# Attention with normed q and k, then a two-layer MLP: where the scratch columns of batch 2's last Newton roots stand

## The chip, the cores and the metric

One core of a Trainium2 chip runs the kernel. The metric is the device time of one launch in microseconds (us); less is better. The engines are named as in the profile: PE (matrix products), PEld (its weight loads), DVE (vector), ACT (activations), POOL, SP (issues transfers). PSUM is the memory into which PE writes its products and from which DVE and ACT read them.

## The reference, cut to what matters

```python
def _attn_ref(q, k, v, g_q, g_k):                    # q, k, v: 8 batches, 12 heads, 448 x 64
    rmsnorm = lambda x, g: x / np.sqrt(np.mean(x * x, axis=-1, keepdims=True) + 1e-06) * g
    q_n, k_n = rmsnorm(q, g_q), rmsnorm(k, g_k)
    scores = 1.0 / np.sqrt(64) * np.matmul(q_n, k_n.transpose(0, 1, 3, 2))
    attn = np.exp(scores - np.max(scores, axis=-1, keepdims=True))
    attn = attn / (np.sum(attn, axis=-1, keepdims=True) + 1e-09)
    return np.matmul(attn, v)

def _moe_ref(x, w_in, w_out):                        # x: 3584 x 768, w_in: 768 x 2048, w_out: 2048 x 768
    h = x @ w_in
    g = 0.5 * h * (1.0 + np.tanh(np.sqrt(2.0 / np.pi) * (h + 0.044715 * h * h * h)))
    return g @ w_out
```

The part around the change is `rmsnorm`: each row of 64 numbers of q and k needs the reciprocal root of its mean square.

## The kernel before, in words

The eight batches go through a software pipeline. For a batch b there are: loads of raw q and k; squares (`square`, L157) and their sums over 64 (`total`, L170); reciprocal roots; the normed q and k (`normed`, L273); their transposes; the attention itself (`attention`, L584, for three chunks c of four heads each, seven steps t per chunk: scores, exponentials, sums, products with v); the first layer (x times w_in and the gelu) and the second layer (g times w_out). In the loop at L925 the pass b does batch b's first layer and then the attention of batch b + 1, between whose steps the second layer of earlier batches is woven in by the hand-written orders `STEADY` and `SECOND` (L571 to L582). All instructions stand in the order in which the code issues them (`manual_schedule`), one in-order queue for each engine.

**The ring of PSUM tiles.** `rounds` holds tiles of 128 x 2 x 512 numbers, that is, two banks of 512 columns. There are two of them at first and four after the attention's start-up (L1022). `pair` (L70) takes the first tile of the list, puts it at the list's end and returns it, so `rounds[-1]` is the tile that was handed out last. Products use the first S = 448 columns of each of the two banks; columns 448 to 511 are not written by them. Every score, sum, product and first-layer step takes its tile from this ring, so a tile taken for something else moves all later ones by a place. `steady()` is true once the ring has four tiles.

**The first layer in steady state** goes by `mm1_turn` (L523). A pair i of 128-column blocks of w_in has one tile of the ring, and its 48 products on 64 x 64 quarters of PE come in two turns (which half of the contraction goes to which bank), and each turn in an early part (cs 0 to 3, 16 products) and a late part (cs 4 and 5, 8 products). When both turns have ended, one gelu on ACT (L543) reads the tile. For batch 1 the order of PE's work is: at the end of `attention(1)` (L678 to L685) the early parts of pairs 0, 1 and 2, both turns, 96 products in all; then in the loop at f == 1 and f == 3 (L991 to L996) the late parts of pairs 0 and 1, 32 products; then at f == 5 (L997 to L1000) the late part of pair 2's turn 1, 8 products, all of pair 3's turn 0, 24 products, and the late part of pair 2's turn 0, 8 products. Pairs 4 to 7 follow, two turns each.

**The last roots.** Most reciprocal roots are made on ACT. `rsqrt_last` (L243) makes those of a batch's last chunk on DVE instead: from 28 mean squares per partition a first guess by integer arithmetic (L255), and three Newton steps of four instructions (L259 to L262), 14 DVE instructions with L254. They run on y (in SBUF), t (in SBUF) and on z and u, two operands of 28 columns that stand in PSUM. It is called twice: for batch 1 before the ring has four tiles (L934), where z and u lie in unused columns of another tile (`oall[0]`), and for batch 2 in steady state (L966), in the loop's slot f == 0 of batch 1's first layer, after the sums of chunk 2 (L965). POOL then makes the normed q and k of chunk 2 with these roots, and SP transposes them.

Before the change, the call for batch 2 takes a tile of the ring for itself, `pair("root")`, and puts z and u side by side in the first columns of its bank 0.

Of the kernel before, what the change touches and what calls it, by code (L numbers as in the profile page):

```python
# [17 lines left out]
def kernel(  # L18
# [12 lines left out]
    B, H, S, D = q.shape  # L31
# [34 lines left out]
    rounds = [  # L66
        ps_t.tile([128, 2, 512], F32, tag=f"t{i}", name=f"t{i}") for i in range(2)
    ]

    def pair(name):  # L70
        rounds.append(rounds.pop(0))
        return rounds[-1]
# [3 lines left out]
    def steady():  # L76

        return bool(late_on)
# [100 lines left out]
    oall = [ps_o.tile([128, 512], F32, tag=f"o{r}", name=f"o{r}") for r in range(2)]  # L179
    roots, places = {}, {}  # L180

    def place(b, c):
        if (b, c) == (0, NCH - 1):
            t = ps_m.tile([128, 512], F32, tag="mm", name="root")[:, :4 * NT]
        else:
            i = c % 2 * 4 * NT
            t = oall[1][:, S + i:S + i + 4 * NT]
        roots["qk", b, c] = t.rearrange("p (n a t) -> p n a t", n=2, a=2)
        for n in range(2):
            roots.setdefault(("qk"[n], b, c), roots["qk", b, c][:, n])  # L190
        return t
# [51 lines left out]
    def rsqrt_last(b):  # L243


        c, flat, m = slice(NCH - 1, NCH), "p c n a t -> p (c n a t)", 4 * NT
        y, ms = rinvs[b][:, c].rearrange(flat), sss[b][:, c].rearrange(flat)
        if steady():
            own, dst = pair("root")[:, 0], y
        else:  # L250
            own, dst = oall[0][:, S:], place(b, 1)
        z, u = own[:, :m], own[:, m:2 * m]
        t = smp.tile([P, NCH * 4 * NT], F32, tag="lg", name="lg")[:, :m]
        nc.vector.tensor_scalar(u, ms, 1.0 / D, 1e-6, op0=ALU.mult, op1=ALU.add)  # L254
        nc.vector.tensor_scalar(  # L255
            y.bitcast(I32), u.bitcast(I32), -0.5, float(0x5F3759DF), op0=ALU.mult, op1=ALU.add
        )
        for i in range(3):
            nc.vector.tensor_copy(z, y)  # L259
            nc.vector.tensor_mul(t, z, y)  # L260
            nc.vector.scalar_tensor_tensor(z, t, -0.5, u, op0=ALU.mult, op1=ALU.mult)
            nc.vector.scalar_tensor_tensor(  # L262
                y if i < 2 else dst, z, 1.5, y, op0=ALU.add, op1=ALU.mult
            )
# [660 lines left out]
    for b in range(B):  # L925
        m1, side, extra, ends = [], [], [], []
        if b == 0:
# [4 lines left out]
                   lambda: normed(1, 0, "k", nc.gpsimd)),  # L932
                  (2, lambda: total(1, 1, "q"), lambda: total(1, 1, "k"),
                   lambda: normed(1, 0, "q", nc.vector), lambda: rsqrt_last(1),  # L934
                   lambda: normed_both(1, 1, nc.vector)),
                  (6, lambda: trans(1, 0, nc.scalar)),
# [23 lines left out]
        elif b + 1 < B:  # L960

            m1.append((0, lambda: gpsimd_waits(ess[b, NCH - 1][:1, 0, 0, :1])))
            for c in range(NCH):
                if b == 1 and c + 1 == NCH:
                    m1 += [(0, lambda: total(2, 2, "q")), (0, lambda: total(2, 2, "k")),  # L965
                           (0, lambda: rsqrt_last(2))]  # L966
                m1 += [(0, lambda c=c: normed_both(b + 1, c, nc.gpsimd)),
                       (4 * c + 4, lambda c=c: transposed(b + 1, c))]
            m1 += [(9, lambda: gain(b + 1, 0)), (14, lambda: gain(b + 1, 1))]
# [13 lines left out]
        for f in range(nf // 2 if b == 0 else nf):  # L983
            i, part = f // 4 * 2, f % 4
# [71 lines left out]
```

## Time and profile before

| what | us |
|---|---|
| median of 3 runs | 391.18 |
| lowest and highest of them | 391.13, 391.48 |
| the profiled execution's own time | 391.23 |
| its span, first to last instruction | 389.2 |
| PE busy in the span | 380.6 |
| ACT busy | 278.7 |
| DVE busy | 235.9 |
| POOL busy | 126.3 |

The span leaves out what lies before the first and behind the last instruction, here 391.23 - 389.2 = 2.0 us. In rows of the timeline stand: start, duration, engine, line, operation, tiles written <- read, shapes, number of instructions, and in brackets the idle time before and what ended it. Rows of the chain have start, duration and what ran. Starts are us from the span's start. PE runs four products on quarters of its array at a time, so the durations of single products overlap.

### The profile page before, as it was taken

The page shows a single profiled execution, that of the slowest core. Times are in us where ns is not written, and L with a number is a line of the kernel's source. Part 1 is how long each engine was busy: PE and PEld are TensorE (multiplying, and loading weights), DVE is VectorE, ACT ScalarE, POOL GpSimd, SP SyncE. Part 2 cuts the span into 40 slices and gives each one's busy share as a digit, 9 for nine tenths or more (in the row PEclk, how much of TensorE's full clock was granted, in tenths as well). Part 3 has the DMA queues.
Part 4 walks back from the last instruction along what each step waited for, and adds up shares of the span by engine and source line. Part 5 has one row for each costly group of instructions (what it writes and reads, how often), then busy time and mean ns, then how long its engine had stood idle before and what let it go on. Part 6 is the DMA issues. An engine that isn't in the chain of part 4 may idle for free.

```text
span 389.2 us, 17542 instructions
## 1 busy us (share of the span) xinstructions
PE 380.6 (98%) x8060; PEld 294.0 (76%) x8060; DVE 235.9 (61%) x366; ACT 278.7 (72%) x353; POOL 126.3 (32%) x110
## 2 busy tenths in 40 slices
PE   7899999999999999999999999999999999999996
PEld 4565577877887788877888788877888778887664
DVE  5998938976596359836589257953598204980010
ACT  6995499767994689757995589946897449944300
POOL 5996506384005440093103740064300900000000
PEclk9999999999999999999999999999999999999999
DMA  8999999999614992379822995159631721120033
GB/s 266 322 231 211 210 230 263 223 200 264 113 44 100 243 213 58 80 132 217 194 65 65 214 227 103 45 110 251 108 80 50 125 44 42 44 65 4 2 83 81
DMA packets 64446, 54.68 MB, mean 141 GB/s; under 512 B 37620, under 2 KB 60020, under 8 KB 64372
## 3 DMA queue, kind: packets, MB, share of 16 engines
q1 hardware_dynamic: 53936, 41.33, 43.8%
q0 software_dynamic: 10128, 11.80, 18.5%
q8 instruction: 63, 1.03, 1.1%
q10 hardware_dynamic: 308, 0.43, 0.4%
q14 instruction: 11, 0.09, 0.1%
HBM read 45.61 MB, written 11.01 MB: 146 GB/s over the span
## 4 chain that ended last, share of the span: by engine, by line
PE 92%; ACT 5%; DMA 1%; issue 1%; DVE 0%; POOL 0%; DVEq 0%
PE t L537 33%; PE t L495 32%; PE t L387 9%; PE t L335 7%; PE t L463 5%; ACT ex L343 4%; PE t L556 4%; DMA rawq<-in_q_dram 1%; PE h L436 1%; PE tp L296 1%; PE o L387 0%; POOL nrmq L278 0%; ACT g L543 0%; DVE ss L173 0%; ACT sq L162 0%
## 5 line engine op out<-in xcount | busy, mean ns | idle before, releaser
L343 ACT ACTIVATE ex<-t,shift 128x896 bf16<-128x896 f32 x168 | 156.2, 1016 | 1.9 <-PE t L335 1.6
L495 PE MATMUL t<-wout,g 64*64 64x384 bf16 (+1 forms) x3456 | 150.6, 305 | 0.0
L537 PE MATMUL t<-xT,win 64*64 64x448 bf16 x2688 | 128.7, 349 | 0.3 <-ACT g L543 0.3
L495 PEld LDWEIGHTS <-g 64*64 64x64 bf16 x3456 | 112.9, 107 | 19.2
L537 PEld LDWEIGHTS <-win 64*64 64x64 bf16 x2688 | 96.6, 107 | 31.0 <-issue 0.5
L543 ACT ACTIVATE g<-t 128x896 bf16<-128x896 f32 x56 | 50.5, 915 | 57.1 <-PE t L537 57.1
L173 DVE TENSOR_REDUCE ss<-sq 128x14 f32<-128x896 f32 (+3 forms) x45 | 44.5, 997 | 51.9 <-ACT sq L162 49.1
L335 PE MATMUL t<-qT,kT 64*64 64x448 bf16 x672 | 58.2, 351 | 1.4 <-ACT ex L343 0.6
L799 POOL COPY mark<-es 1x1 bf16<-1x1 bf16 x7 | 1.2, 177 | 132.0 <-DVE es L362 128.3
L355 DVE TENSOR_TENSOR es<-ex 128x1792 bf16<-128x1792 bf16 x20 | 21.2, 1061 | 33.0 <-ACT ex L343 33.0
L278 POOL TENSOR_TENSOR nrmq<-rawq,rinv 128x896 bf16<-128x896 f32 (+1 forms) x21 | 34.9, 1660 | 18.6 <-ACT rinv L205 11.0
L278 POOL TENSOR_TENSOR nrmk<-rawk,rinv 128x896 bf16<-128x896 f32 (+1 forms) x21 | 34.4, 1640 | 0.0
L387 PE MATMUL t<-ex,vb 64*64 64x448 bf16 x588 | 31.9, 350 | 0.0
L335 PEld LDWEIGHTS <-kT 64*64 64x64 bf16 x672 | 25.5, 106 | 7.3 <-DVE kT L305 1.2
L397 DVE STREAM_TRANSPOSE st<-t 128x448 f32<-128x448 f32 x42 | 24.7, 626 | 9.7 <-PE t L387 9.7
L387 PEld LDWEIGHTS <-vb 64*64 64x64 bf16 x672 | 23.5, 107 | 7.3 <-issue 1.0
L409 DVE STREAM_TRANSPOSE rb<-rc 128x896 f32<-128x896 f32 (+1 forms) x25 | 26.7, 1068 | 0.3
L705 DVE COPY osb<-t 128x384 f32<-128x384 f32 (+1 forms) x4 | 2.0, 507 | 35.2 <-PE t L463 35.2
L422 DVE TENSOR_TENSOR xT<-t,rb 128x896 bf16<-128x896 f32 x21 | 22.8, 1087 | 0.8
L164 POOL TENSOR_TENSOR sq<-rawq 128x896 f32<-128x896 f32 (+1 forms) x9 | 13.6, 1513 | 28.6 <-DVE ss L173 27.3
L513 ACT COPY osb<-t 128x768 f32<-128x768 f32 (+1 forms) x18 | 12.6, 701 | 13.9 <-PE t L495 13.9
L358 DVE TENSOR_TENSOR es<-es,ex 128x1792 bf16<-128x1792 bf16 x20 | 21.3, 1063 | 0.7 <-ACT ex L343 0.6
(103 smaller groups left out, 313.5 us busy)
## 6 DMA issues: line engine op xcount, KB each, us to landing
rawq<-in_q_dram SPq DMA_DIRECT2D x22, 448.0 KB, 5.0
rawk<-in_k_dram SPq DMA_DIRECT2D x22, 448.0 KB, 5.8
out_dram<-osb SPq DMA_DIRECT2D x42, 192.0 KB, 2.7
vb<-in_v_dram POOLq DMA_DIRECT2D x6, 672.0 KB, 7.3
win<-in_moe_w_in_dram POOLq DMA_DIRECT2D x8, 384.0 KB, 10.8
wout<-in_moe_w_out_dram POOLq DMA_DIRECT2D x3, 768.0 KB, 17.1
out_dram<-osb SPq DMA_DIRECT2D x24, 96.0 KB, 3.7
vb<-in_v_dram POOLq DMA_DIRECT2D x2, 448.0 KB, 15.5
```

What stands on the lines that cost most here:

```text
L173: nc.vector.reduce_sum(sss[b][:, seat(b, c), "qk".index(n), hs, ts], squares(b, c, n, hs, ts), axis=AX.X)
L278: eng.tensor_mul(nrms[n, b, c][:, ts].rearrange("p t a d -> p a t d"), raws[n, b, c][:, :, ts], root[:, :, ts].to_broadcast([P, 2, m, D]),)
L335: nc.tensor.matmul(sc[r * R:(r + 1) * R, a, :S], kT[rs, c, t, r], qT[b][rs, c, :, r], start=True, stop=True,)
L343: nc.scalar.activation(exs[b, c][:, t], scs.pop((b, c, t))[:, :, :S], AF.Exp, scale=scale, bias=shift)
L358: nc.vector.tensor_add(es, es, ex[:, 4:6])
L387: nc.tensor.matmul(o[r][a * D:(a + 1) * D], vb[b % 2][rs, 2 * c + a, i] if what else ones[rs], es[i][rs, a], start=(i == 0), stop=(i == n ...
L397: nc.vector.transpose(st[:, r].rearrange("p a b -> p (a b)"), o[r])
L409: nc.vector.transpose(oas["rb"][:, rs].rearrange("p r s -> p (r s)"), rc.to_broadcast([128, (rs.stop - rs.start) * m, 32]),)
L422: nc.vector.tensor_mul(xT[b][:, 2 * c:2 * c + 2], oas["o", c, 1][:, :, :S], oas["rb"])
L495: mm = nc.tensor.matmul(o[a * R:(a + 1) * R, bank, :hi - lo], g[rs, f, at:at + R], wout[rs, f, lo:hi], start=(n == 0), stop=(n == len(step ...
L537: mm = nc.tensor.matmul(h[a * R:(a + 1) * R, j, :S], win[rs, c, at:at + R], xT[b][rs, c], start=begin and c == cs[0], stop=end and c == cs ...
L543: nc.scalar.activation(g[:, 2 * i:2 * i + 2, (b % 2) * S:(b % 2 + 1) * S], h[:, :, :S], AF.Gelu_apprx_tanh,)
```

## The change

In `rsqrt_last`, for the call in steady state: no tile is taken from the ring. z stands in columns 448 to 475 of bank 0 and u in columns 448 to 475 of bank 1 of `rounds[-1]`, the tile that was handed out last. The ring is not turned, so the tile that the roots had taken before goes to the next user. The other branch computes the same places as before. The 14 DVE instructions, their number and their shapes stay. The change adds one line, so the lines behind it have numbers greater by one in the changed kernel.

```diff
         if steady():
-            own, dst = pair("root")[:, 0], y
+            z, u = (rounds[-1][:, i, S:S + m] for i in range(2))
+            dst = y
         else:
-            own, dst = oall[0][:, S:], place(b, 1)
-        z, u = own[:, :m], own[:, m:2 * m]
+            z, u = oall[0][:, S:S + m], oall[0][:, S + m:S + 2 * m]
+            dst = place(b, 1)
         t = smp.tile([P, NCH * 4 * NT], F32, tag="lg", name="lg")[:, :m]
         nc.vector.tensor_scalar(u, ms, 1.0 / D, 1e-6, op0=ALU.mult, op1=ALU.add)
```

## Prediction

> **What bounds the kernel now.** I read the page first: its head, the busy shares and the chain that ended last.
>
> ```profile
> span 389.2 us, 17542 instructions
> PE 380.6 (98%) x8060; PEld 294.0 (76%) x8060; DVE 235.9 (61%) x366; ACT 278.7 (72%) x353; POOL 126.3 (32%) x110
> PE 92%; ACT 5%; DMA 1%; issue 1%; DVE 0%; POOL 0%; DVEq 0%
> ```
>
> PE is busy for 98% of the span and makes 92% of the chain. So a microsecond that PE loses counts in full if it isn't given back later, and work that DVE loses counts only through PE. That is an average, so the next view is PE's own waits from 82 us on, and then a window that runs from 82.62 us to the end.
>
> ```profile
> PE t L537 <- ACT g L543: 0.3, 1, 0.3
> 82.62:389.15 306.53, 302.87 (x6848) 241.90 (x6847) 169.45 (x228) 214.42 (x266) 75.64 (x53) 1.00 0.53 114
> 385.49:389.15 3.66, 0.00 (x0) 0.00 (x0) 0.36 (x1) 0.00 (x0) 0.00 (x0) 1.00 0.41 108
> ```
>
> In the first row are the total, the number and the longest of PE's waits: one wait, of 0.3 us, for a gelu, in the whole rest of the kernel. In the other two, the columns behind the length are the busy time of PE, PEld, DVE, ACT and POOL, then the granted clock, the DMA share and GB/s. PE is busy for 302.87 us from 82.62 us on and for none of the last 3.66 us: 306.53 - 3.66 = 302.87, so it has no idle time between 82.62 and 385.49 us. A delay of PE at 82 us meets nothing later that could absorb it. The one wait and the change are in the same place, the first layer of batch 1, so I went there next, in narrow windows of the timeline.
>
> ```profile
> 81.60 0.58 PE L537 MATMUL t<-xT,win 64*64 64x448 bf16 x8
> 81.65 0.92 ACT L543 ACTIVATE g<-t 128x896 bf16<-128x896 f32 x1 [2.45 <-PE t L537]
> 81.79 0.58 PE L537 MATMUL t<-xT,win 64*64 64x448 bf16 x8
> ...
> 81.98 0.39 PE L537 MATMUL t<-xT,win 64*64 64x448 bf16 x4
> ...
> 82.62 0.38 PE L537 MATMUL t<-xT,win 64*64 64x448 bf16 x4 [0.26 <-ACT g L543]
> ```
>
> Products start in groups of four, one on each quarter of PE, and a group follows the last by 0.19 us: 81.60, 81.79, 81.98. Each lasts 0.39 us, so two groups overlap. The next group should start at 81.98 + 0.19 = 82.17 and starts at 82.62: **PE loses 0.45 us**, though only 0.26 us of it shows as idle. It is pair 3, whose tile is the one that pair 0 had, and pair 0's gelu ends at 81.65 + 0.92 = 82.57. PE starts 0.05 us later.
>
> The run of first-layer products before that wait has 136 of them:
>
> ```profile
> 75.73 6.63 PE L537 MATMUL t<-xT,win 64*64 64x448 bf16 x136
> ```
>
> By the code these are the 96 early ones of pairs 0, 1 and 2, the 32 late ones of pairs 0 and 1, and last the 8 of pair 2's turn 1: 96 + 32 + 8 = 136. The last two groups, which start at **81.79** and 81.98, are therefore pair 2's turn 1.
>
> **The change part by part.** *The ring isn't turned.* Pair 3 gets the tile that the roots had before, and no gelu stands in its way. This removes the wait of 0.45 us. The tiles of pairs 4 and 5 also come one user later and pair 6 now takes pair 2's tile, behind pair 2's gelu; by the code 120 products lie between pair 2's last and pair 6's first, so by 0.048 us each (6.63 / 136, rounded down) there are 5.8 us for a gelu of 0.92 us. From pair 7 on the ring is the same up to names. Cost of all this: nothing.
>
> *The scratch moves to a tile in use.* `rounds[-1]` is then pair 2's tile, handed out at the end of `attention(1)`, with its early parts done and its late parts to come. Its columns 448 to 475 are written by no product. What decides is whether the program orders DVE and PE nevertheless. The listing of the built programs answers that. In the old one pair 2's turn 1 waits for nothing and pair 3 waits for ACT; in the new one:
>
> ```
> 2410 L538 Matmult t3_893<-xT_1310,win_119 64x448 [waits DVE_49]
> ...
> 2426 L538 Matmult t1_101<-xT_1310,win_119 64x448
> ```
>
> The first row is the first of pair 2's last 8 products (t3), the second the first product of pair 3 (t1), which now waits for nothing. The count for which the first waits is that of the last Newton instruction, L262 (L263 in the new numbering). The first Newton instruction in turn waits for pair 2's early products.
>
> That the order is by bank and not by column is what the Trainium skill asks for ("PSUM — Partial Sum Buffer", section "PSUM bank collisions raise a hardware error"): two engines in one bank and one quarter of its partitions at once are an error even at different columns, so it says to guard "by bank × quadrant, not by address". It speaks against this change: columns that no product uses are no separate place. By columns alone the sum would be -0.45 us, by the bank it is the one below. No run here shows the collision itself; the built program follows the rule.
>
> *When do the roots end?* The timeline of DVE:
>
> ```profile
> 80.17 1.07 DVE L173 TENSOR_REDUCE ss<-sq 128x14 f32<-128x896 f32 x1
> 81.28 0.19 DVE L254 TENSOR_SCALAR t<-ss 128x28 f32<-128x28 f32 x1
> 81.51 0.19 DVE L255 TENSOR_SCALAR rinv<-t 128x28 int32<-128x28 int32 x1
> ...
> 84.19 0.18 DVE L262 SCALAR_TENSOR_TENSOR rinv<-t,rinv 128x28 f32<-128x28 f32 x1
> ```
>
> The 14 instructions start 0.22 us apart, from 81.28 to 84.19, and the last ends at 84.37. They can't start earlier: the sum over the last squares ends at 80.17 + 1.07 = 81.24. Nor does their own new wait delay them: pair 2's early products are the 96th of 136 and end at about 75.73 + 96 x 0.048 + 0.3 = 80.6 us, 0.7 us before 81.28. A second wait in front of one instruction costs DVE's queue an extra semaphore instruction; L422 has such ones:
>
> ```profile
> L422 DVEq EVENT_SEMAPHORE  x8: 21/21/848, 64.0 to 347.5; - x8
> ```
>
> 0.02 us, the median. That z and u are in two banks instead of one is not shown in the trace. The same instructions with their operands in another PSUM tile, for batch 1, are the nearest rows:
>
> ```profile
> L254 DVE TENSOR_SCALAR o<-ss x1: 181/181/181, 42.5 to 42.5; 128x28 f32<-128x28 f32 x1
> L254 DVE TENSOR_SCALAR t<-ss x1: 191/191/191, 81.3 to 81.3; 128x28 f32<-128x28 f32 x1
> ```
>
> 10 ns between two places in PSUM. For 14 instructions that is up to 0.14 us either way; I take 0, as the other forms differ by nothing like as much, and keep -0.14 and +0.14 for the range.
>
> *What the new wait costs.* The time from the end of a DVE instruction to a product that waited for it is in these rows:
>
> ```profile
> 17.36 0.56 DVE L278 TENSOR_TENSOR nrmk<-rawk,o 128x384 bf16<-128x384 f32 x1
> ...
> 17.97 0.23 PE L296 MATMUL tp<-ident,nrmk 128*128 128x128 bf16 x1 [0.48 <-DVE nrmk L278]
> ```
>
> 17.97 - 17.92 = 0.05 us. So pair 2's last 8 products start at 84.37 + 0.02 + 0.05 = 84.44 us instead of 81.79. PE's queue is in order, so everything behind them on PE waits too. Pair 3 follows two groups later, at 84.44 + 2 x 0.19 = 84.82, instead of 82.62. **The sum: 84.82 - 82.62 = +2.20 us** (2.65 us of stall, less the 0.45 us that the ring gave back). From there PE's order is the old one without idle time, so it ends 2.20 us later, and with it the last copies and stores.
>
> What else is late: pair 2's gelu (old start 84.38 us) and, behind it in ACT's queue, the squares for batch 3. ACT has time: it is busy for 214.42 of the 306.53 us. What hangs on DVE and POOL alone, the normed q and k of batch 2's last chunk and their transposes, stays where it is and is 2.2 us early against PE. That opens no new wait, and there was none on PE to close.
>
> So the profiled execution's 391.23 us become 393.43. It stands 0.05 us above the median of the runs shown, 391.18; against that the forecast is 393.4 us.
>
> **The rivals.**
>
> *The wait doesn't hold PE (the other side).* If the roots were through before PE reaches pair 2's last 8 products, or the wait were met otherwise, only the ring's gain would be left: 391.2 - 0.45 = 390.8 us. It decides at 81.79 us: the last Newton instruction would have to end 2.6 us earlier than it did. Against it stands that the first one starts at 81.28, behind a sum that ends 0.04 us before, in a chain of 0.22 us steps. For it: nothing but a wait that counts something else than I read. I give it 3 in 100. It comes out within 0.2%.
>
> *PE comes back at a lower clock.* The stall leaves PE idle from 81.98 us, the end of the group of 81.60, to 84.44, that is 2.46 us. If the granted clock fell for it, the products behind would go at half pace for a while. Taken as long as the longest idle time in the rows above, 3.66 us, half pace loses 1.83 us: 393.4 + 1.8 = 395.2 us. Against it: in the row from 385.49 us PE is idle for 3.66 us at a granted clock of 1.00 throughout. I give it 5 in 100. The Trainium skill ("TensorE: Matmul & The Clock Gate", section "Why this matters for your kernels") warns of idle gaps over about 3 us, as one window of 3.4 us without work halves the clock; by its figure the loss would be an estimated 1.7 us. Our gap is under that, and the trace's row leans the same way.
>
> *Part is given back.* Products behind the stall could go closer together, if small waits are now hidden under overlapping products. The chain of work shows their pace before and behind the old wait:
>
> ```profile
> 75.93 5.70 PE t L537 x120
> ...
> 82.62 11.92 PE t L537 x248
> ```
>
> 47.5 and 48.1 ns each: 0.15 us at most in this stage, and PE's other stages have no idle time either. With 0.3 us given back it is 393.1 us. I give it 7 in 100; it lies in the range.
>
> **How the numbers follow.** Forecast 85 in 100, 393.4 us. Its own range is 393.0 to 393.9: 0.14 us for the place of the operands, 0.35 us for the distance between the lowest and highest run shown. The range goes from 392.8, where some is given back, to 394.2, part of the way to a lower clock. A measurement of this kernel can tell about 0.2% from no change, 0.8 us. Slower by more than that: the forecast, the lower clock and the part given back, 85 + 5 + 7 = 97, less 1 for a return large enough to hide it: 96. The 4 that are left are that return and the case without a wait; 3 of them lie within 0.2% of no change, and 1 is for a gain by more, faster.
>
> **What would show it.** Right: in the changed profile PE has one wait of about 2.5 us at 82 us, of L538 for DVE's L263; pair 3 starts near 84.8 us without a wait for a gelu; the 14 DVE instructions stand between 81.3 and 84.4 us with the same lengths; from there on PE has no idle time and ends near 387.7 us, in a span near 391.4; the clock stays at 1.00. Wrong: PE reaches 82.17 us without a stop (no wait held it), or the Newton chain itself starts later or takes longer than 3.1 us, or PE's products behind the stall run at a pace other than 48 ns, or PE waits again for ACT or DMA behind 85 us.

## The result, and the profile after

The changed kernel takes **393.62 us** (median of 4 runs, 393.21 to 394.08) against 391.16 us (4 runs, 391.13 to 391.48): ratio **1.0061**, 95% interval 1.0044 to 1.0079. It is slower by 2.5 us, and the whole interval is above 0.2%. The profiled execution took 393.56 us, 2.33 us more than the profiled one before, and its span grew by 391.5 - 389.2 = 2.3 us.

The page of the changed kernel, its head, the busy shares and the chain that ended last:

```profile
span 391.5 us, 17544 instructions
PE 381.1 (97%) x8060; PEld 293.3 (75%) x8060; DVE 236.2 (60%) x366; ACT 278.9 (71%) x353; POOL 126.3 (32%) x110
PE 89%; ACT 5%; DVE 3%; DMA 1%; issue 1%; POOL 0%; DVEq 0%
```

The work is the same: as many products, DVE and ACT instructions. Two instructions more are the semaphore waits that precede the first DVE instruction of the roots and the gelu of pair 2. DVE, which had 0% of the chain, now makes 3% of it. PE's waits from 20 us on:

```profile
PE t L538 <- DVE rinv L263: 2.5, 1, 2.5
PE t L336 <- ACT ex L344: 0.3, 1, 0.3
```

The wait for the gelu (L537 for L543, now L538 for L544) is gone, and one for the last Newton instruction stands in its place. The timeline around it:

```profile
79.22 2.07 DVE L173 TENSOR_REDUCE ss<-sq 128x14 f32<-128x896 f32 x2
...
81.40 0.19 DVE L255 TENSOR_SCALAR t<-ss 128x28 f32<-128x28 f32 x1
...
84.30 0.18 DVE L263 SCALAR_TENSOR_TENSOR rinv<-t,rinv 128x28 f32<-128x28 f32 x1
84.54 2.81 PE L538 MATMUL t<-xT,win 64*64 64x448 bf16 x53 [2.52 <-DVE rinv L263]
```

The 14 instructions of the roots start 0.22 us apart as before. The last ends at 84.48, and pair 2's last 8 products start 0.06 us later. The bracket says that PE had been idle for 2.52 us. The chain shows what follows:

```profile
84.08 0.20 DVE t L262
84.30 0.20 DVE rinv L263
84.54 12.30 PE t L538 x256
96.84 0.81 PE t L496 x20
```

256 products in 12.30 us, 48 ns each, and then the second layer: pair 3 starts without a wait, and the pace is the old one. A window from there to the end and one behind PE's last product (busy times of PE, PEld, DVE, ACT, POOL, then granted clock, DMA share, GB/s):

```profile
84.54:391.45 306.91, 303.25 (x6856) 241.27 (x6855) 167.97 (x220) 213.20 (x264) 75.45 (x52) 1.00 0.51 113
387.79:391.45 3.66, 0.00 (x0) 0.00 (x0) 0.36 (x1) 0.00 (x0) 0.00 (x0) 0.81 0.41 108
```

306.91 - 3.66 = 303.25: no idle time of PE in between, so nothing gives the loss back. The second row has a clock of 0.81 where the same idle stretch at the end of the kernel before showed 1.00. That turns out to matter.

### The profile page after: what moved, and what is told of

Read it like the earlier page. It is cut to its first block, busy times and chain, and to the rows that moved or that the text cites. A ratio compares the mean times of both kernels' runs of the same rounds, so it can differ in the third digit from the quotient of the medians.

```text
span 391.5 us, 17544 instructions
## 1 busy us (share of the span) xinstructions
PE 381.1 (97%) x8060; PEld 293.3 (75%) x8060; DVE 236.2 (60%) x366; ACT 278.9 (71%) x353; POOL 126.3 (32%) x110
## 4 chain that ended last, share of the span: by engine, by line
PE 89%; ACT 5%; DVE 3%; DMA 1%; issue 1%; POOL 0%; DVEq 0%
PE t L496 32%; PE t L538 31%; PE t L388 8%; PE t L336 7%; PE t L464 5%; ACT ex L344 4%; PE t L557 4%; DVE ss L173 1%; DMA rawq<-in_q_dram 1%; PE h L437 1%; DVE xT L423 1%; PE tp L297 1%; PE o L388 0%; DVE rb L410 0%; DVE st L398 0%
## 5 line engine op out<-in xcount | busy, mean ns | idle before, releaser
L538 PE MATMUL t<-xT,win 64*64 64x448 bf16 x2688 | 128.7, 349 | 2.5 <-DVE rinv L263 2.5
L538 PEld LDWEIGHTS <-win 64*64 64x64 bf16 x2688 | 96.1, 107 | 33.7 <-issue 2.8
L544 ACT ACTIVATE g<-t 128x896 bf16<-128x896 f32 x56 | 50.5, 915 | 59.3 <-PE t L538 59.3
L336 PE MATMUL t<-qT,kT 64*64 64x448 bf16 x672 | 58.1, 351 | 1.4 <-ACT ex L344 0.6
L336 PEld LDWEIGHTS <-kT 64*64 64x64 bf16 x672 | 25.4, 106 | 7.5 <-DVE kT L306 1.5
```

The costliest lines, as they stand in the source:

```text
L336: nc.tensor.matmul(sc[r * R:(r + 1) * R, a, :S], kT[rs, c, t, r], qT[b][rs, c, :, r], start=True, stop=True,)
L538: mm = nc.tensor.matmul(h[a * R:(a + 1) * R, j, :S], win[rs, c, at:at + R], xT[b][rs, c], start=begin and c == cs[0], stop=end and c == cs ...
L544: nc.scalar.activation(g[:, 2 * i:2 * i + 2, (b % 2) * S:(b % 2 + 1) * S], h[:, :, :S], AF.Gelu_apprx_tanh,)
```

## The experiments

Some executions, of the kernel before too, take one to three microseconds longer than the rest without a lower clock. In two profiled executions (pair 3 ahead, and the changed kernel once more) the trace has a late transfer: DVE waits 1.7 to 1.8 us, until about 63.5 us, for a transpose into kT, and PE then waits 1.5 us in L336 for DVE's L142. That the others have the same cause is not shown. Medians are given with the lowest time where this blurs them. The ratios come with their intervals and are not the quotients of the two medians, from which they can differ a little.

**The place of the scratch alone.** The ring is turned as before the change:

```diff
             z, u = (rounds[-1][:, i, S:S + m] for i in range(2))
+            pair("root")
```

Expected: 

> The changed kernel, but the ring is turned by one tile after the roots have taken their place, as it was before the change: only the place of the scratch differs from the kernel before. Theory (PE is held at pair 2's last 8 products until the last Newton step ends): the gain of the ring, 0.45 us, lies behind the stall and can't be seen, so the time is that of the changed kernel, 393.4 to 393.7 us, with one wait of PE of 2.5 us. Rival one (the loss comes from the new order of tiles in the ring): 391.2 us. Rival two (stall and ring add up): 393.6 + 0.45 = 394.1 us.

Measured: 394.15 us (393.52 to 395.31, 6 executions) against 391.30, ratio 1.0067 (1.0043 to 1.0091). Four executions had a mean granted clock of 0.998 to 1.000 and took 393.52 to 394.52 us; two had 0.994 and 0.995 and took 394.98 and 395.31. The first group fits the wait, with the ring's gain hidden behind it (one execution, of 394.52 us, lies above the expectation, nearer to rival two; the trace has one wait of 2.5 us and none for the gelu beside it); the ring's order is not the cause. The second group was in no theory. Its profiled execution, in windows cut at the changes of the clock:

```profile
81.55:84.96 3.41, 0.90 (x24) 0.48 (x19) 2.47 (x14) 2.19 (x3) 1.65 (x2) 1.00 0.89 233
84.96:88.37 3.41, 3.41 (x44) 2.22 (x40) 0.00 (x0) 0.24 (x1) 2.98 (x2) 0.50 1.16 290
88.37:91.79 3.42, 3.42 (x80) 2.57 (x75) 1.60 (x2) 2.87 (x5) 0.00 (x0) 1.00 1.14 250
```

The column behind POOL is the granted clock: **0.50 for 3.41 us** right after the stall, with 44 products in it where the next window of the same length has 80. The chain of the same execution gives the price:

```profile
84.52 13.98 PE t L539 x256
```

13.98 - 12.30 = 1.68 us for the same 256 products.

**The ring alone.** The scratch goes to SBUF:

```diff
-            z, u = (rounds[-1][:, i, S:S + m] for i in range(2))
+            z, u = (smp.tile([P, m], F32, tag=n, name=n) for n in ("zz", "uu"))
```

Expected: 

> The ring's part alone: no tile is taken from the ring, and z and u are two small tiles in SBUF. Theory: no instruction of PE waits for the roots, and pair 3 doesn't wait for pair 0's gelu: 391.2 - 0.4 = 390.8 us, PE without a wait behind 20 us. Rival (the order of tiles in the ring costs the time): 393.6 us. If the Newton steps are slower in SBUF beside POOL (0.2 to 0.4 us each instead of 0.22), the roots come up to 2.5 us later and nothing waits for them on PE: still 390.8 us.

Measured: 391.09 us (lowest 390.51, 12 executions) against 391.30 (lowest 391.04), ratio 0.9995 (0.9976 to 1.0014): no loss, and the gain is not told from no change by the times. The trace shows it. PE's only wait behind 20 us, and the chain:

```profile
PE t L336 <- ACT ex L344: 0.3, 1, 0.3
```

```profile
75.78 18.16 PE t L538 x384
93.94 0.81 PE t L496 x20
```

The whole first layer of batch 1, 384 products, goes without a stop at 47 ns each, in 18.16 us. In the kernel before it went from 75.93 to 82.62 + 11.92 = 94.54 us by its chain, 18.61 us: the ring's part is 0.45 us.

**The scratch in the next tile of the ring** (pair 3's) instead of the last:

```diff
-            z, u = (rounds[-1][:, i, S:S + m] for i in range(2))
+            z, u = (rounds[0][:, i, S:S + m] for i in range(2))
```

Expected: 

> The changed kernel with the scratch columns in the tile that the ring hands out next (pair 3's) instead of the one handed out last. Theory (a wait by tile, whatever the columns): now pair 3's first product waits for the last Newton step; PE gets to it at 82.2 us and is let go at 84.5 us, where it started at 82.62 before: 391.2 + 1.9 = 393.1 us, the stall 0.4 us shorter than in the changed kernel. Rival (only a tile with half-made sums in it is held): 390.8 us. Rival (the ring's order): 393.6 us.

Measured: 394.77 us (394.53 to 394.92, 5 executions) against 391.30, ratio 1.0079 (1.0057 to 1.0101): missed by 1.7 us. The wait is as expected, 2.1 us (first fence: PE's waits, the row for L538), and so the tile that is held needn't have half-made sums in it. What the expectation lacks is the clock, at 0.995 or 0.996 in four of the five executions:

```profile
PE t L538 <- DVE rinv L263: 2.1, 1, 2.1
```

```profile
82.26:85.67 3.41, 1.34 (x32) 0.95 (x31) 1.82 (x10) 1.60 (x3) 1.72 (x2) 1.00 0.90 231
85.67:89.09 3.42, 3.42 (x44) 2.29 (x40) 1.08 (x1) 2.15 (x4) 2.19 (x2) 0.50 1.37 193
```

```profile
84.45 13.61 PE t L538 x248
```

The kernel before makes these 248 products in 11.92 us: 1.69 us are the clock's, and without them the profiled execution's 394.53 would be 392.84, near the 393.1 expected. The fifth execution took 394.92 us at a clock of 0.999; it has no profile, and why it took so long stays open.

**Pair 3 ahead of pair 2's rest:**

```diff
-                mm1_turn(b, 2, 1, late)
                 mm1_turn(b, 3, 0, range(HP), begin=True)
+                mm1_turn(b, 3, 1, range(HP), end=True)
+                mm1_turn(b, 2, 1, late)
                 mm1_turn(b, 2, 0, late, end=True)
...
-            elif part == 3:
+            elif part == 3 and (b, f) != (1, 7):
```

Expected: 

> The changed kernel, with all 48 products of pair 3 issued ahead of pair 2's last 16. Theory (the release is a fixed time, set by DVE): PE gets to pair 2's products 48 x 0.048 = 2.3 us later, at 84.1 us, and is let go at 84.5 us: a stall of 0.4 us, as long as the old wait for the gelu, so 391.2 us. Rival (the stall has its own length of 2.5 us wherever it stands, or the ring's order costs the time): 393.6 us.

Measured: 391.56 us (eleven executions 391.35 to 391.84, one 393.11) against 391.30, ratio 0.9998 (0.9985 to 1.0011). With 2.3 us of other products in front, the stall of 2.5 us is gone: it is a fixed time at which PE is let go. The profiled execution is the one of 393.11, with the late transfer, which moves everything behind it; this is its row among PE's waits:

```profile
PE t L336 <- DVE rawk L142: 1.5, 1, 1.5
```

PE's products in this kernel, in narrow windows of the timeline:

```profile
84.39 0.39 PE L538 MATMUL t<-xT,win 64*64 64x448 bf16 x4
84.84 0.38 PE L538 MATMUL t<-xT,win 64*64 64x448 bf16 x4
85.62 0.55 PE L538 MATMUL t<-xT,win 64*64 64x448 bf16 x8
86.15 0.38 PE L538 MATMUL t<-xT,win 64*64 64x448 bf16 x4
86.34 0.38 PE L538 MATMUL t<-xT,win 64*64 64x448 bf16 x4
86.79 0.38 PE L538 MATMUL t<-xT,win 64*64 64x448 bf16 x4
```

Groups should follow by 0.19 us. Twice they follow by 0.45 (84.39 to 84.84, 86.34 to 86.79): there a pair changes its turn with no other pair's products between, and the second turn waits until the first is finished (`follows` in `mm1_turn` orders them), for 0.26 us each. In between, at 86.15, is what is left of the wait for the roots. So this order buys the stall back, and pays for it in turns.

**Two, and four, Newton steps** in the changed kernel (with two, the third step of the roots is left out), and four in the kernel before. The diff is that for two steps; the other two kernels have 4 in the place of the 2 in its first line:

```diff
-        for i in range(3):
+        for i in range(2 if steady() else 3):
...
-                y if i < 2 else dst, z, 1.5, y, op0=ALU.add, op1=ALU.mult
+                y if i < 2 or steady() else dst, z, 1.5, y, op0=ALU.add, op1=ALU.mult
```

Expected of two: 

> The changed kernel with two Newton steps instead of three for batch 2's last roots (the third step is left out). Theory of the wait: PE is let go four instructions of 0.22 us earlier, 0.89 us, so 393.5 - 0.9 = 392.6 us, PE idle for 1.6 us. Theory of the clock (a span of 3.41 us that is more than about half idle is followed by as long a span at half clock, as in the traces of e1_turned and e3_nexttile): 1.6 us is under half of 3.41, so no execution pays for it, and the runs lie close together. Rival (any stall of PE lowers the clock): 392.6 + 1.5 = 394.1 us. Rival (the stall isn't what costs the time): 393.6 us.

Expected of four: 

> The changed kernel with four Newton steps. Theory of the wait alone: 393.5 + 0.9 = 394.4 us. With the theory of the clock: PE is idle for 3.4 us, as long as one span of the clock's, so wherever those spans begin one of them is at least half idle, and most executions have 3.4 us at half clock, which cost 1.4 us more (as between the runs of e1_turned with and without): 395.8 us. Rival (the stall isn't what costs the time): 393.6 us.

Expected of four in the kernel before: 

> The kernel before the change with four Newton steps instead of three for the same roots. Theory: PE waits for none of these instructions, and the normed q and k of that chunk have time, so nothing changes: 391.2 us. Rival (the length of the roots' chain costs time by way of POOL and the transposes, whatever tile they use): 392.1 us.

Measured: with two 392.62 us against 391.26 (12 executions, all at a clock of 0.998 or more), ratio 1.0032 (1.0015 to 1.0049); with four 396.22 us (5 executions, all at 0.994 to 0.996), ratio 1.0129 (1.0096 to 1.0161); the kernel before with four 391.27 against 391.26 us, ratio 0.9993 (0.9977 to 1.001). The same four instructions cost 0.9 us of waiting (PE's wait is 1.6, 2.5 and 3.4 us with two, three and four steps) or nothing, by whether PE waits for them. The waits of PE in the first two, and the windows of the clock:

```profile
PE t L538 <- DVE rinv L263: 1.6, 1, 1.6
```

```profile
81.08:84.49 3.41, 1.79 (x43) 1.12 (x36) 2.30 (x11) 2.19 (x3) 2.54 (x3) 1.00 0.77 166
84.49:87.90 3.41, 3.41 (x80) 2.57 (x76) 0.50 (x1) 1.91 (x4) 2.78 (x2) 1.00 1.51 280
```

```profile
PE t L538 <- DVE rinv L263: 3.4, 1, 3.4
```

```profile
82.15:85.57 3.42, 0.24 (x8) 0.19 (x11) 2.65 (x15) 1.63 (x3) 0.77 (x2) 1.00 0.88 230
85.57:88.98 3.41, 3.41 (x44) 2.23 (x40) 0.00 (x0) 0.00 (x0) 3.18 (x2) 0.50 1.16 284
```

With four steps the expectation was 0.4 us short. It took the clock at 1.4 us, from whole executions of the first experiment, where the chain gives 1.7 (14.01 us for the 256 products, less 12.30); the other 0.1 us is not accounted for.

**A shorter chain in SBUF.** u is one small tile in SBUF; z and the copies into it are gone:

```diff
-            z, u = (rounds[-1][:, i, S:S + m] for i in range(2))
+            u = smp.tile([P, m], F32, tag="uu", name="uu")
...
-            nc.vector.tensor_copy(z, y)
-            nc.vector.tensor_mul(t, z, y)
-            nc.vector.scalar_tensor_tensor(z, t, -0.5, u, op0=ALU.mult, op1=ALU.mult)
+            nc.vector.tensor_mul(t, y, y)
+            nc.vector.scalar_tensor_tensor(t, t, -0.5, u, op0=ALU.mult, op1=ALU.mult)
```

Expected: 

> No tile is taken from the ring; u stands in SBUF, z and the copies into it are gone, so a Newton step is three instructions. Theory: as e2_sbuf, no wait of PE behind 20 us, 390.8 us, by the 0.42 us that the old wait for the gelu cost; the three DVE instructions fewer bring nothing. Rival (the shorter chain brings something): 390.1 us.

Measured: 390.91 us (lowest 390.25, 12 executions) against 391.26 (lowest 390.69), ratio 0.9984 (0.9966 to 1.0003). It is the lowest median here, 0.35 us under the kernel before, as the 0.42 us of the wait that it lacks would have it, but the interval touches no change.

**The changed kernel once more.**

Expected: 

> The changed kernel once more, unaltered, for the share of its executions that pay for the clock. PE is idle for 2.5 us. By the traces so far a span of 3.41 us in which PE is busy for 1.3 us or less is followed by as long a span at half clock, one in which it is busy for 1.7 us or more isn't, and these spans begin at another point in each execution. Such a stall leaves under 1.3 to 1.7 us of work in some span for 0.5 to 0.8 of all starting points: so of 6 or more executions some have a mean clock of 0.994 to 0.996 and take 395.0 to 395.3 us, the others 0.998 or more and 393.2 to 393.8 us. Rival (the changed kernel doesn't pay for the clock, only the others did): all at 0.998 or more, 393.2 to 394.1 us.

Measured: 394.46 us, ratio 1.0066 (1.0044 to 1.0088), in two groups: 393.54, 393.57 and 393.63 at 0.998 or more, and 395.29, 395.46 and 396.99 at 0.994 or 0.995, the last with a late transfer too. So the changed kernel has two times, 393.5 and 395.3 us. The profiled execution, that of 396.99 us, shows the cause of the second in this kernel itself:

```profile
83.74:87.16 3.42, 0.91 (x23) 0.71 (x23) 2.10 (x12) 1.87 (x3) 1.66 (x2) 1.00 0.94 273
87.16:90.57 3.41, 3.41 (x44) 2.23 (x38) 0.00 (x0) 1.14 (x2) 2.52 (x2) 0.50 1.15 283
```

```profile
86.27 13.98 PE t L538 x256
```

The stall is the same 2.5 us, a window at half clock follows, and the 256 products take 1.68 us longer than in the first profile. The four executions behind the result above were all without it: 3 of 10 had it, fewer than the 0.5 to 0.8 of the expectation; ten are few, and why stays open.

## Why the prediction was right, point by point

- *The wait is real, though no product uses the columns*: right. PE idles for 2.52 us at L538 for DVE's L263. Moving the scratch to SBUF removes it, moving it to the next tile moves it, and a longer or shorter chain of roots lengthens or shortens it by the 0.9 us of four instructions.
- *When the roots end*: forecast 84.37 + 0.02, measured 84.48. Upstream the trace lies 0.04 us later. The extra wait was sized at 0.02 us, the semaphore instruction's own row. Between the sum's end (79.22 + 2.07 = 81.29) and L255 (81.40) are now 0.11 us; before there were 0.03 to 0.04. The term is 0.07 to 0.08 us. Two banks instead of one cost nothing: the same 0.22 us a step.
- *From there to the product*: forecast 0.05 us, measured 0.06.
- *What the ring gives back*: 0.45 us, right in size by the chains of the kernel before and of the one with the scratch in SBUF, and hidden by the stall as the first experiment shows: with the ring turned PE has the same wait.
- *The sum*: +2.20 us forecast for the profiled execution, 2.33 measured. With the extra wait at 0.08 it would have been 2.26, and 0.04 lie upstream. In the range, 393.4 less 0.14 and 0.35 is 392.9 and not 393.0; nothing hangs on it.
- *No clock loss*: **the step that failed.** The prediction took one idle stretch of 3.66 us at the end of one trace, at 1.00, as evidence that 2.5 us are harmless, and gave the lower clock 5 in 100 at 395.2 us. The price was near: 395.3. The chance was not: 3 of 10 executions of the changed kernel had it, and 2 of 6 of the first experiment's with the same stall. The stretch didn't show what it was taken for, and the trace of the kernel before says so when it is cut where its clock changes:

```profile
385.78:389.15 3.38, 0.00 (x0) 0.00 (x0) 0.16 (x1) 0.00 (x0) 0.00 (x0) 1.00 0.41 109
389.19:391.47 2.28, 0.00 (x0) 0.00 (x0) 0.00 (x0) 0.00 (x0) 0.00 (x0) 0.50 0.01 4
```

The clock did fall, at 389.19 us, when the window without work, which began at 385.78, was over, and the last instruction had ended 0.04 us before. The changed kernel's end, with the same 3.66 us, shows 0.81 only because the fall came at 390.06 us there, before its last instruction at 391.45. The forecast's 393.4 us is the time of the executions that escape the half clock; that the result's four all did is luck.
- *Part given back*: nothing was; PE has no idle time behind the stall, and 48 ns per product as before.

## What to carry to other kernels

Free columns of a PSUM tile were no free place while another engine still had that tile to write: the program ordered the two engines whatever the columns, so a slow helper on one engine became a wait of the engine that is the bound. Whether it orders them by the tile or by the bank is not told apart here, as z and u lay in both banks of the tile. Before putting scratch there, look where in the bound engine's queue the tile is next touched, and compare that time with the end of the helper; SBUF (391.09 against 391.30 us), or other work put in front (391.56), cost nothing that the times tell. And price a stall of PE of two microseconds or more at its length plus, in a share of the executions, a window at half clock, which cost 1.7 us here. No execution had one behind a stall of 1.6 us, of 12; 5 of 16 had one behind 2.5 us, 4 of 5 behind 2.1 us and 5 of 5 behind 3.4 us.

## What the runs showed of the hardware that was not expected

The granted clock goes by windows of 3.41 us that begin at another point in each execution (84.96, 85.67, 85.57 and 87.16 us are such borders in four traces, and each spell at 0.50 that PE worked through lasted one window). Where a trace has no such spell, the borders are counted back in steps of 3.413 us from the one at the kernel's end, 390.06 us in the changed kernel's first trace. PE busy for 0.24, 0.90, 0.91 or 1.34 us of one was followed by half clock in the next, with PE at work all the time; 1.79 us was not, and neither was 1.73 us in the changed kernel's own trace:

```profile
82.86:86.27 3.41, 1.73 (x37) 1.29 (x39) 1.39 (x8) 1.02 (x2) 1.65 (x1) 1.00 0.90 276
86.27:89.69 3.42, 3.42 (x80) 2.61 (x76) 1.09 (x1) 3.02 (x5) 1.69 (x2) 1.00 1.12 289
```

At the end of a kernel it shows too. In the kernel before with four steps, 1.50 us of work in a window were enough for full clock in the next, in which PE had nothing to do:

```profile
384.13:387.54 3.41, 1.50 (x19) 1.27 (x16) 0.36 (x1) 0.32 (x1) 0.00 (x0) 1.00 0.39 102
387.54:390.95 3.41, 0.00 (x0) 0.00 (x0) 0.00 (x0) 0.00 (x0) 0.00 (x0) 1.00 0.05 14
```

So by these traces the border lies between 1.34 and 1.50 us of work in a window. The Trainium skill ("TensorE: Matmul & The Clock Gate", section "What's actually happening") has the free-running window of 3413 ns, and the traces agree; it asks for at least one idle window before the clock falls, and here the measurement differs: a stall of 2.1 us did it, with PE busy for 39% of the window.

In SBUF the first instruction of the roots took 1.57 us instead of 0.19, beside a POOL instruction that began just before it and ended with it (timeline of the kernel with the scratch in SBUF):

```profile
80.99 1.68 POOL L279 TENSOR_TENSOR nrmk<-rawk,rinv 128x896 bf16<-128x896 f32 x1
81.14 1.57 DVE L255 TENSOR_SCALAR uu<-ss 128x28 f32<-128x28 f32 x1
```

The Trainium skill ("Advanced Engine Details and Errata", section "Mode Summary") says that the second SBUF port of the vector engine is shared with GpSimd, and that GpSimd's instructions and vector instructions in a mode with two ports block each other. The rows agree with a block, but do not show which ports the instruction used. It cost nothing here, as PE no longer waited for the roots.
